# Sliding-window attention with own keys for each half block of 64 queries

## Chip, cores and metric

The kernel runs on one core of a Trainium2 chip. The metric is the device time of one execution in microseconds (us); lower is better. The time before is 763.34 us, the median of three runs (763.32 to 763.45).

## What is computed

An attention stage is followed by two mixture-of-experts layers. The inputs have 2 batches, 8 heads, 768 positions and a head dimension of 64. Each query sees the first 8 positions of its sequence (the global keys) and the 96 positions up to itself (the local keys), with a bias that grows with the distance:

```python
is_global = pos[None, :] < int(n_global)
is_local = (rel >= 0) & (rel < int(n_local))
dist = np.where(is_global & ~is_local, float(n_local), np.abs(rel))
scores = scale * q @ k.T - slopes[:, None, None] * dist
scores = np.where(is_global | is_local, scores, -1e9)
a = np.exp(scores - scores.max(-1)); a = a / (a.sum(-1) + 1e-9)
x = (a @ v)                       # then as rows of 8 * 64
idx = argmax(normalized(x) @ normalized(emb).T / tau)
x = gate[idx] * relu(x @ w1[idx]) @ w2[idx]          # layer 1, 8 experts
out = sum_e p[:, e] * relu(x @ w1[e]) @ w2[e]        # layer 2, 4 experts
```

## The kernel before

**Blocks.** The 1536 rows are 12 blocks (`T`) of 128 queries, six per batch. The 8 heads of a block are 4 pairs, called `n` in the code: 4 x t + 0 to 3, with the two heads `j` = 0, 1 of a pair on partitions 0 to 63 and 64 to 127 of queries and keys. The first block of a batch has only its own 128 keys. Every other block works on a window of 240: 96 local keys before the block and 16 slots for the global keys (`WG` = 112 together), and its own 128.

**One pair of one block** goes through these functions. `scores` (L541) multiplies queries by keys on TensorE, one matmul of 128 queries by 240 keys for each head. `maximum` (L554, VectorE) scales, adds the bias `biasw` and leaves the negated result in `aa` and the row's extreme in `nm`. `expo` (L560, ScalarE) takes the exponential and its row sum. `flip` (L568) transposes `aa` on TensorE in 128 by 128 squares, two for each head, four into one PSUM bank of the pool `ps_a`, which is then copied to SBUF as `ats` (L570, by ScalarE or VectorE as the call says). `av` (L582) multiplies by the values: for each head one matmul with the 112 keys of the earlier part (`vwin`) and one with the 128 own keys (`v`), accumulated in `o`, a bank of the pool `ps_o`.

**Finishing a block.** `fin0` copies `o` to `os` on ScalarE (L237). `fin_l` (L257) multiplies two pairs at a time by `idn`, which holds for every pair an identity and the expert embeddings side by side (144 columns): this puts the rows back in order and gives the expert logits, both in the one bank of the pool `ps_l`, called `lp`. VectorE reads it in `over_sums` (`lh`, L275) and `rows_x` (`xall`, L287), dividing by the row sums; `end_x` does both for one half. `choose` finds the expert of each row in small steps, `count` (L310, L311) and `fin2` (L317, L320) find each row's slot in the expert's list, and `scatter` (L324) writes the rows with an indirect DMA of the POOL queue to `xs` in DRAM, which must have been zeroed (`zero_fill`, L493, from `zt`).

**Order.** Each engine works through its own queue in program order, and the order is written out by hand in the loop over t at the end of the attention part: while block t has its flips, finishing of t-1 and weighted values, the scores of block t+2 follow on TensorE, and maximum and exponentials of block t+1 run on VectorE and ScalarE. PSUM's eight banks are divided among pools: `ps_o` 1, `ps_l` 1, `ps_a` 2, `ps_s` (scores) 4.

**Loads.** SyncE's queue issues them, also in program order: `load_v(t+2)` at the head of block t (L404 to L408), `load_kq(t+4)` (L389, L391), zero fills in blocks 1, 2, 4 and 5, and `load_to` (L86), which brings the first layer's weights (`raw`). `split_low_pieces` and `split_half` then split these weights in two parts, `wh` on ScalarE (L138, L141) and `wl` on POOL (L107) in this stage. `put_globals` (L396) copies the 16 global key slots behind each block's keys.

**The opening and the end.** `build_dist` (L476 to L478) and `build_biasw` (L482) make the distance and the eight biases on VectorE before block 1's maxima; `warm` issues matmuls that nobody reads. In the last block the lists of the last blocks are placed, 256 rows of the first expert are loaded from `xs` as `xe` (L699), and TensorE starts the first layer with `first_rows` (L360) and `add_rows` (L364).

Of the kernel before, what the change touches and what calls it, by code (L numbers as in the profile page):

```python
# [22 lines left out]
P = 128  # L23
GW = 16
PW = 96
WG = GW + PW
WIN = WG + 128
# [9 lines left out]
def tile_attention_moe_moe(ctx: ExitStack, tc: tile.TileContext, q, k, v, n_global, n_local,  # L37
# [169 lines left out]
    idn = cp.tile([P, NP, 2 * D + 2 * NE], F32, name="idn")  # L207
# [40 lines left out]
    HH, NX = H // 2, 2 * D + 2 * NE  # L248
    lps, pps = {}, {}

    def fin_l(t_, i, pool=None, place=None):


        pt = (pool or pl.l).tile([P, HP * NX + NE], F32, tag="at" if pool else "l", name="lp")
        lps[t_, i] = pt[:, 0:HP * NX].rearrange("p (a n) -> p a n", a=HP)
        for p_ in range(HP):
            nc.tensor.matmul(lps[t_, i][:, p_, :], osb[t_][:, i * HP + p_, :], idn[:, i * HP + p_, :],  # L257
                             start=True, stop=True)
        if place is not None:
            count(place, pt[:, HP * NX:])  # L260
# [8 lines left out]
    def over_sums(t_, i):  # L269

        rs, lh = osb[t_, 2]
        rp = rs.rearrange("p (i a j) -> p i a j", i=2, j=2)[:, i]
        lp = lps[t_, i]
        pt = lp[:, :, 2 * D:].rearrange("p a (j e) -> p a j e", j=2)
        nc.vector.tensor_tensor(lh[:, i * HH:(i + 1) * HH, :].rearrange("p (a j) e -> p a j e", j=2), pt,  # L275
                                rp.unsqueeze(3).to_broadcast([P, HP, 2, NE]), ALU.mult)

    def rows_x(t_, i, scalar=False):
        rs, _ = osb[t_, 2]
        rp = rs.rearrange("p (i a j) -> p i a j", i=2, j=2)[:, i]  # L280
        x_ = xall[:, t_, :].rearrange("p (i a j d) -> p i a j d", i=2, j=2, d=D)[:, i]
        pt = lps.pop((t_, i))[:, :, 0:2 * D].rearrange("p a (j d) -> p a j d", j=2)
        if scalar:
            for h in range(HH):
                nc.scalar.activation(x_[:, h // 2, h % 2], pt[:, h // 2, h % 2], AF.Copy, scale=rs[:, i * HH + h:i * HH + h + 1])
        else:
            nc.vector.tensor_tensor(x_, pt, rp.unsqueeze(3).to_broadcast([P, HP, 2, D]), ALU.mult)  # L287
# [79 lines left out]
    with ExitStack() as at:  # L367
# [4 lines left out]
        ap6 = at.enter_context(tc.tile_pool(name="ap6", bufs=6))  # L372
# [4 lines left out]
        pl.sb, pl.l = ap2, ps_l  # L377
# [4 lines left out]
        SEG = P + GW  # L382
        kp = [ap1.tile([P, NP, TB * SEG], F32, name=f"k{b}") for b in range(B)]
        vwin = [ap1.tile([WG, DM], F32, name=f"vwin{i}") for i in range(NB)]
        vt, qt = {}, {}
# [7 lines left out]
        def put_globals(b, i0, i1, copy=nc.gpsimd.tensor_copy):  # L393

            seg = kp[b].rearrange("p a (i c) -> p a i c", c=SEG)
            copy(seg[:, :, i0:i1, P:SEG],  # L396
                                  kp[b][:, :, 0:GW].unsqueeze(2).to_broadcast([P, NP, i1 - i0, GW]))

        def load_v(t_):
            b, i = divmod(t_, TB)  # L400
            s0 = i * P
            vw = vwin[t_ % NB]
            vt[t_] = ap3.tile([P, DM], F32, tag="v", name="v")
            nc.sync.dma_start(out=vt[t_], in_=v[b, s0:s0 + P, :])  # L404
            if i:
                nc.sync.dma_start(out=vw[0:PW], in_=v[b, s0 - PW:s0, :])
            if 1 <= i <= NB:
                nc.sync.dma_start(out=vw[PW:WG], in_=v[b, 0:GW, :])  # L408


        it32 = ap1.tile([P, WIN], I32, name="it32")
# [16 lines left out]
        nc.gpsimd.iota(it32[:, 0:PW], [[-1, PW]], base=PW, channel_multiplier=1)  # L428
# [175 lines left out]
        def end_x(t_, i):  # L604
            if t_ >= 0:
# [7 lines left out]
                if i:  # L613
                    choose(t_)
# [856 lines left out]
```

## Time and profile before

| what | value |
|---|---|
| median of three runs | 763.34 us |
| the profiled execution | 764.26 us, its span 762.5 us |
| granted TensorE clock, mean | 0.997 |
| busy share PE, DVE, ACT, POOL | 98, 75, 56, 46% |
| attention | from the start to about 92 us |
| the two layers | the rest |

PE is TensorE, PEld its weight loads, DVE VectorE, ACT ScalarE, POOL GpSimd, SP SyncE, which issues most DMAs. The span is the stretch that the profiler's records cover; the execution's own time is 1.76 us longer. The chain of waits is the chain of work that ended last, followed back from the last instruction. Rows of a timeline give start, duration, engine, line, operation, the tile written and the one read, shapes, and how many instructions the row holds; a bracket at the end gives the idle time before it and what ended that.

### The profile page before, as it was taken

The page shows a single profiled execution, that of the slowest core. Times are in us where ns is not written, and L with a number is a line of the kernel's source. Part 1 is how long each engine was busy: PE and PEld are TensorE (multiplying, and loading weights), DVE is VectorE, ACT ScalarE, POOL GpSimd, SP SyncE. Part 2 cuts the span into 40 slices and gives each one's busy share as a digit, 9 for nine tenths or more (in the row PEclk, how much of TensorE's full clock was granted, in tenths as well). Part 3 has the DMA queues.
Part 4 walks back from the last instruction along what each step waited for, and adds up shares of the span by engine and source line. Part 5 has one row for each costly group of instructions (what it writes and reads, how often), then busy time and mean ns, then how long its engine had stood idle before and what let it go on. Part 6 is the DMA issues. An engine that isn't in the chain of part 4 may idle for free.

```text
span 762.5 us, 16427 instructions
## 1 busy us (share of the span) xinstructions
PE 749.4 (98%) x6268; PEld 728.0 (95%) x6268; DVE 568.3 (75%) x1197; ACT 424.3 (56%) x865; POOL 349.2 (46%) x316
## 2 busy tenths in 40 slices
PE   8999999999999999999999999999999999999995
PEld 4888899999999999999999999999999999999995
DVE  6888676877979678777667678777677677766765
ACT  7899667766766565663444454444454344345331
POOL 2026450070004574676467366267357356555325
PEclk9999999999999999999999999999999999999998
DMA  7995467677797874566566566466557556644532
GB/s 230 324 304 203 136 218 237 213 235 245 259 325 258 314 268 157 210 251 238 186 249 248 193 245 238 171 236 245 194 183 264 194 205 229 223 170 173 213 132 96
DMA packets 46757, 169.89 MB, mean 223 GB/s; under 512 B 5368, under 2 KB 13576, under 8 KB 38208
## 3 DMA queue, kind: packets, MB, share of 16 engines
q1 hardware_dynamic: 44224, 162.11, 60.7%
q0 software_dynamic: 2416, 6.39, 2.3%
q8 instruction: 66, 1.08, 0.5%
q14 instruction: 35, 0.29, 0.1%
q10 hardware_dynamic: 16, 0.02, 0.0%
HBM read 146.96 MB, written 21.54 MB: 221 GB/s over the span
## 4 chain that ended last, share of the span: by engine, by line
PE 87%; DVE 4%; issue 4%; POOL 2%; ACT 1%; DMA 1%; POOLq 0%; SPq 0%; ACTq 0%; DVEq 0%
PE h L1091 10%; PE h L1092 10%; PE h L1093 10%; PE y L1172 6%; PE y L1170 6%; PE y L1171 6%; PE h L1019 3%; PE h L1020 3%; PE h L1021 3%; PE ya L1172 3%; PE ya L1171 3%; PE ya L1170 3%; PE ya L1039 3%; PE y L1039 3%; PE s L541 2%
## 5 line engine op out<-in xcount | busy, mean ns | idle before, releaser
L1091 PE MATMUL h<-xo,wt 128*128 128x256 f32 x672 | 190.4, 283 | 0.2 <-ACT h L1124 0.2
L1093 PE MATMUL h<-xo,wt 128*128 128x256 f32 x672 | 190.2, 283 | 0.0
L1092 PE MATMUL h<-xo,wt 128*128 128x256 f32 x672 | 190.2, 283 | 0.0
L157 POOL TENSOR_TENSOR wt<-raw,wt 128x512 fp32r<-128x512 f32 x75 | 101.6, 1355 | 142.8 <-ACT wt L156 142.8
L1091 PEld LDWEIGHTS h<-xo,wt 128*128 128x128 f32 x672 | 129.0, 192 | 0.5 <-ACT h L1124 0.4
L1092 PEld LDWEIGHTS h<-xo,wt 128*128 128x128 f32 x672 | 129.0, 192 | 0.0
L1093 PEld LDWEIGHTS h<-xo,wt 128*128 128x128 f32 x672 | 129.0, 192 | 0.0
L1072 DVE SCALAR_TENSOR_TENSOR xall<-y,rsb,xall 128x256 f32<-128x256 f32 x196 | 85.8, 478 | 52.8 <-PE y L1172 52.6
L1172 PE MATMUL y<-wt,hp 128*128 128x256 f32 x416 | 117.9, 283 | 0.1
L1170 PE MATMUL y<-wt,hp 128*128 128x256 f32 x416 | 117.7, 283 | 0.0
L1171 PE MATMUL y<-wt,hp 128*128 128x256 f32 x416 | 117.7, 283 | 0.0
L1096 ACT ACTIVATE hp<-hf 128x512 fp32r<-128x512 f32 x120 | 75.2, 628 | 57.8 <-DVE hf L1105 57.1
L1099 DVE TENSOR_TENSOR hp<-hf,hp 128x512 fp32r<-128x512 f32 x93 | 90.4, 976 | 0.0
L1172 PEld LDWEIGHTS y<-wt,hp 128*128 128x128 f32 x416 | 79.8, 192 | 0.5 <-DVE hp L1102 0.5
L1170 PEld LDWEIGHTS y<-wt,hp 128*128 128x128 f32 x416 | 79.9, 192 | 0.0
L1171 PEld LDWEIGHTS y<-wt,hp 128*128 128x128 f32 x416 | 79.9, 192 | 0.0
L94 DVE TENSOR_TENSOR wl<-raw,wh 128x1024 fp32r<-128x1024 f32 x60 | 76.8, 1295 | 0.1
L1138 ACT ACTIVATE hf<-h 128x512 f32<-128x512 f32 x24 | 14.3, 598 | 106.9 <-DVE h L1137 106.9
L124 ACT ACTIVATE wh<-raw 128x1024 fp32r<-128x1024 f32 x59 | 62.1, 1059 | 17.1 <-DMA raw<-in_moe_w_dram 13.2
L1170 PE MATMUL ya<-wt,hp 128*128 128x256 f32 x244 | 69.3, 284 | 0.1
L1171 PE MATMUL ya<-wt,hp 128*128 128x256 f32 x244 | 69.0, 283 | 0.0
L1172 PE MATMUL ya<-wt,hp 128*128 128x256 f32 x244 | 69.0, 283 | 0.0
(248 smaller groups left out, 1919.2 us busy)
## 6 DMA issues: line engine op xcount, KB each, us to landing
raw<-in_moe_w_dram SPq DMA_DIRECT2D x96, 512.0 KB, 4.6
xo<-xd SPq DMA_DIRECT2D x44, 1024.0 KB, 5.6
xo<-xd SPq DMA_DIRECT2D x22, 1536.0 KB, 6.2
xd<-xo SPq DMA_DIRECT2D x14, 512.0 KB, 5.1
xs<-zt SPq DMA_DIRECT2D x4, 1024.0 KB, 6.5
xr<-xs SPq DMA_DIRECT2D x14, 256.0 KB, 5.4
v<-in_v_dram SPq DMA_DIRECT2D x12, 256.0 KB, 4.5
k<-in_k_dram SPq DMA_DIRECT2D x11, 256.0 KB, 5.3
```

The costliest lines, as they stand in the source:

```text
L94: eng.tensor_tensor(lo, r, hi.bitcast(F32), ALU.subtract)
L124: nc.scalar.activation(hi, r, AF.Copy)
L157: eng.tensor_tensor(t[:, 1], src, t[:, 0].bitcast(F32), ALU.subtract)
L1072: nc.vector.scalar_tensor_tensor(a_, src, w_, a_, ALU.mult, ALU.add)
L1091: nc.tensor.matmul(pt[:, i], wh[:, d, ws], xh_[:, d], start=new and i == d == 0, stop=False, skip_group_check=True)
L1092: nc.tensor.matmul(pt[:, i], wh[:, d, ws], xl_[:, d], start=False, stop=False, skip_group_check=True)
L1093: nc.tensor.matmul(pt[:, i], wl[:, d, ws], xh_[:, d], start=False, stop=d == 1, skip_group_check=True)
L1096: nc.scalar.activation(parts[i][0], src, func)
L1099: eng.tensor_tensor(parts[i][1], src, parts[i][0].bitcast(F32), ALU.subtract)
L1170: nc.tensor.matmul(pt, hh[:, f, ts_], wh[:, f], start=new and f == 0, stop=False, skip_group_check=True)
L1171: nc.tensor.matmul(pt, hh[:, f, ts_], wl[:, f], start=False, stop=False, skip_group_check=True)
L1172: nc.tensor.matmul(pt, hl[:, f, ts_], wh[:, f], start=False, stop=f == 1, skip_group_check=True)
```

## The change

Each block of 128 queries is divided into two halves `g` of 64 (`HB`), and each half has its own window of 176 keys (`WIN` = 112 + 64): 112 earlier and global ones and its own 64. The second half's earlier keys are the first half's own 64, the 32 keys before them (the tail, `TL`) and the globals.

- **Scores**: tiles of 64 queries by up to 176 keys instead of 128 by 240; each pair has 9 matmuls (before 2), some of which cover two pieces. A tail of 32 keys is copied behind each block's keys by `put_tail` on POOL.
- **Bias**: `build_dist` has 13 VectorE instructions instead of 3, and makes the window for both heads, whose columns are in different order.
- **Flips**: `aa` of a pair is one row of 2 x 176 columns, so that the own keys of both heads lie together. Three squares are flipped for a pair instead of four: one for each head's 112, and one with both heads' own 64. `aa` lies in six fixed tiles.
- **Weighted values**: for each half and head one matmul of 64 x 64 with the 112 rows of `vh`, and one with the 128 rows of `vo`. `vo` holds the block's own values, each head on its half of the partitions and zeros on the other; `own_keys` copies it on POOL from `vh`, two copies of 64 x 512 a block.
- **Loads of values**: into three tiles `vh`, in two to five pieces a block; `load_v(t+2)` is called behind block t's `av` instead of at its head.
- **Finishing**: `fin_l` is called once a block, at its head, with 16 matmuls of 72 columns on tiles of 64 x 64 (before 4 of 144). The even heads go to `lp`, which is now a bank of `ps_a`, the odd ones to `lq`, a bank of `ps_o`'s tag. The pools are `ps_o` 1, `ps_a` 3, `ps_s` 4. `end_x` is one call, the odd heads first.
- **Order**: the maximum of `m1`'s second head is ahead of `end_x` and its exponential behind it; in odd blocks the copy of `n2`'s flip is VectorE's.

The two layers are not touched. The core of the diff:

```diff
-WIN = WG + 128
+HB = 64
+TL = PW - HB
+WIN = WG + HB
...
-    def fin_l(t_, i, pool=None, place=None):
-        pt = (pool or pl.l).tile([P, HP * NX + NE], F32, tag="at" if pool else "l", name="lp")
-        for p_ in range(HP):
-            nc.tensor.matmul(lps[t_, i][:, p_, :], osb[t_][:, i * HP + p_, :], idn[:, i * HP + p_, :],
-                             start=True, stop=True)
+    def fin_l(t_, place=None):
+        pt = [pool.tile([P, 512], F32, tag=tag, name=n) for (pool, tag), n in ((pl.l, "lp"), (pl.o, "lq"))]
+        for p_ in range(NP):
+            for j in range(2):
+                r0 = slice(D * j, D * j + D)
+                for g in range(2):
+                    c0 = slice(D * g, D * g + D)
+                    nc.tensor.matmul(lps[t_][j][c0, p_, :], osb[t_][r0, p_, c0], idn[r0, p_, :], start=True, stop=True)
...
-        ps_l = at.enter_context(tc.tile_pool(name="ps_l", bufs=1, space=PSUM))
-        ps_a = at.enter_context(tc.tile_pool(name="ps_a", bufs=2, space=PSUM))
+        ps_a = at.enter_context(tc.tile_pool(name="ps_a", bufs=3, space=PSUM))
...
+    def put_tail(t_):
+        b, i = divmod(t_, TB)
+        if i < TB - 1:
+            c0 = i * SEG
+            nc.gpsimd.tensor_copy(kp[b][:, :, c0 + P + GW:c0 + SEG], kp[b][:, :, c0 + HB - TL:c0 + HB])
...
+    def own_keys(t_):
+        if t_ % TB:
+            src = vh[t_ % NB][0:HB].rearrange("k g (a j d) -> k j g a d", j=2, d=D)
+            for j in range(2):
+                nc.gpsimd.tensor_copy(vo[HB * j:HB * j + HB, j], src[:, j])
...
-                    nc.tensor.matmul(score(n, j), qt[t_][r0, p_, :], kp[b][r0, p_, c1 - (WIN if i else P):c1], start=True, stop=True)
+                    elif j == 0:
+                        todo[j] = [(0, 0, c0 + HB, WIN), (1, HB, c0 + P - TL, GW + TL), (1, 0, c1, P)]
+                    else:
+                        todo[j] = [(0, HB, c0 + HB, WG), (1, P, c0 + P - TL, GW + TL), (0, 0, c1, HB),
+                                   (1, 0, c1 + HB, HB), (1, HB, c1, HB)]
+                while todo[0] or todo[1]:
+                    for j in range(2):
+                        for g, o, c, w in todo[j][0:2]:
...
+                            nc.tensor.matmul(s_, qt[t_][r0, p_, gs], k_, start=True, stop=True)
+                        del todo[j][0:2]
...
+                for j, c in enumerate((0, WIN + HB, WG)):
+                    nc.tensor.transpose(pt[:, j, :], a_[:, c:c + P], ident)
+                copy(s_, pt[:, 0:3, :])
...
+            for g in range(2):
+                gs = slice(HB * g, HB * g + HB)
+                for j in range(2):
+                    nc.tensor.matmul(o_[j][:, gs], vh[(t_ - 1 + g) % NB][0:WG, 1 - g, hs[j]], s_[0:WG, j, gs], start=True, stop=False)
+                for j in range(2):
+                    nc.tensor.matmul(o_[j][:, gs], vo[:, j, g, p_, :], s_[:, 2, gs], start=False, stop=True)
...
-            if 1 <= t_ and t_ + 2 < T:
-                load_v(t_ + 2)
+            if t_ + 2 < T:
+                put_tail(t_ + 2)
...
-                end_l(t_ - 1, 0)
+                end_l(t_ - 1)
                 top(m0, 0)
...
                 top(m1, 0)
-                flip(n2, nc.scalar.copy)
-                top(m1, 1)
-                end_x(t_ - 1, 0)
+                if t_ < T - 1:
+                    maximum(m1, 1)
+                end_x(t_ - 1)
...
+                flip(n2, nc.vector.tensor_copy if t_ % 2 else nc.scalar.copy)
+                if t_ < T - 1:
+                    expo(m1, 1)
                 tops(m2)
                 flip(n3, nc.vector.tensor_copy)
-                end_l(t_ - 1, 1)
                 tops(m3)
-                end_x(t_ - 1, 1)
             if t_:
                 for n in (n0, n1, n2, n3):
                     av(n)
...
+            if t_ and t_ + 2 < T:
+                load_v(t_ + 2)
+            if t_ + 1 < T:
+                own_keys(t_ + 1)
             if t_:
                 scores(2 * t_ + 4)
                 scores(2 * t_ + 5)
```

How it moves instructions is seen in three places. On TensorE one block before, from its scores to the count of the finished block (`s` scores, `at` flips, `lp` finishing):

```order
L541 MATMUL s<-k_127,q 128x240 x8
L568 MATMUL at<-ident,aa 128x128 x8
L257 MATMUL lp<-idn,os 128x144 x2
L568 MATMUL at<-ident,aa 128x128 x8
L257 MATMUL lp<-idn,os 128x144 x2
L310 LDWEIGHTS tri
L310 MATMUL lp<-oh,tri 128x8
```

TensorE in the same place now, first one pair's scores and the start of the finishing:

```order
L594 MATMUL s<-k_121,q 64x176
L594 MATMUL s<-k_121,q 64x48
L594 MATMUL s<-k_121,q 64x112
L594 MATMUL s<-k_121,q 64x48
L594 MATMUL s<-k_121,q 64x2x64
L594 MATMUL s<-k_121,q 64x64 x3
L262 MATMUL lp<-idn,os 64x72 x2
L262 MATMUL lq<-idn,os 64x72 x2
```

and from the finishing's end to the first weighted values (`o`):

```order
L312 LDWEIGHTS tri
L312 MATMUL lp<-oh,tri 128x8
L313 LDWEIGHTS ones
L313 MATMUL lp<-cum,ones 128x8
L623 MATMUL at<-ident,aa_130 128x128 x3
L623 MATMUL at<-ident,aa_131 128x128 x3
L623 MATMUL at<-ident,aa_132 128x128 x3
L623 MATMUL at<-ident,aa_133 128x128 x3
L646 MATMUL o<-ats,vh_124 64x64 x2
L648 MATMUL o<-ats,vo 64x64 x2
```

Both halves of the finishing and the count now stand ahead of all flips, and there are three flips for a pair. On POOL around the scatters of block 6, before:

```order
L324 DMA xs<-xall,slot 2048x512 x2
L107 TENSOR_TENSOR wl<-raw,wh 128x256 x4
L320 CAST slot<-base 128x1
L298 TENSOR_TENSOR cum<-cum,oh 128x8
L324 DMA xs<-xall,slot 2048x512 x2
```

and now:

```order
L430 COPY vo<-vh_124 64x512 x2
L326 DMA xs<-xall,slot 2048x512 x2
L109 TENSOR_TENSOR wl<-raw,wh 128x256 x4
L407 COPY k_122<-k_122 128x4x32
L322 CAST slot<-base 128x1
L300 TENSOR_TENSOR cum<-cum,oh 128x8
L430 COPY vo<-vh_125 64x512 x2
L326 DMA xs<-xall,slot 2048x512 x2
```

The copies for block 8's own keys (the second `vo`) stand behind two scatters and four weight pieces. On SyncE's queue in block 1, with what each instruction waits for (PE is TensorE), before:

```order
L404 DMA v<-in_v_dram 128x512 [waits DMAHW5_49,PE_49]
L406 DMA vwin_129<-in_v_dram 96x512 [waits DMAHW6_49]
L408 DMA vwin_129<-in_v_dram 16x512 [waits DMAHW7_49]
L389 DMA k_127<-in_k_dram 128x4x128 [waits DMAHW0_49]
L391 DMA q<-in_q_dram 128x512 [waits DMAHW1_49]
L493 DMA xs<-zt 512x1x512 [waits DMAHW2_49,DVE_49]
L86 DMA raw<-in_moe_w_dram 128x1024 [waits DMAHW3_49]
```

and now:

```order
L417 DMA vh_123<-in_v_dram 64x2x512 [waits DMAHW5_49,PE_49]
L418 DMA vh_123<-in_v_dram 32x512 [waits DMAHW6_49]
L420 DMA vh_123<-in_v_dram 32x512 [waits DMAHW7_49]
L392 DMA k_121<-in_k_dram 128x4x128 [waits DMAHW0_49]
L394 DMA q<-in_q_dram 128x512 [waits DMAHW1_49]
L531 DMA xs<-zt 512x1x512 [waits DMAHW2_49,DVE_49]
L88 DMA raw<-in_moe_w_dram 128x1024 [waits DMAHW3_49]
```

The order of the queue is the same, but the first load now waits for TensorE's weighted values of block 1 where it waited for those of block 0.

## Rows read from the trace of the kernel before

**Rows 1.** Windows: stretch, us, busy us (count) of each engine, PEclk, DMA share, GB/s.

```profile
30.00:40.00 10.00, 10.00 (x111) 8.81 (x108) 8.29 (x47) 9.39 (x32) 1.47 (x6) 1.00 0.92 304
```

**Rows 2.** Chain of waits in attention: start us, us, what.

```profile
30.71 1.82 PE s L541 x16
32.53 1.02 PE at L568 x8
33.56 0.49 PE lp L257 x4
34.05 0.95 PE at L568 x8
...
35.52 1.91 PE o L582 x32
37.43 1.82 PE s L541 x16
...
48.41 1.91 PE o L582 x32
...
67.27 1.91 PE o L582 x32
```

**Rows 3.** Timeline of VectorE in a full block.

```profile
43.14 0.19 DVE L275 TENSOR_TENSOR lh<-lp,rs 128x32 f32<-128x32 f32 x1
...
43.58 0.16 DVE L317 CUSTOM_DVE_ANT_0 g<-lp,oh 128x8 f32<-128x8 f32 x1
```

**Rows 4.** Timeline of VectorE in the opening.

```profile
9.21 0.34 DVE L476 TENSOR_SCALAR far<-rel,nf 128x240 f32<-128x240 f32 x1
...
10.03 0.23 DVE L478 TENSOR_SCALAR dd<-gf,nf 128x16 f32<-128x16 f32 x1
...
11.89 0.41 DVE L554 CUSTOM_DVE_ANT_0 aa<-s,biasw 128x240 f32<-128x240 f32 x1 [0.58 <-PE s L541]
```

**Rows 5.** Timeline of TensorE: block 0's second half of `fin_l`.

```profile
21.36 0.73 PE L257 MATMUL lp<-idn,os 128*128 128x144 f32 x4 [0.76 <-DVE xall L287]
```

**Rows 6.** SyncE's queue in block 1, then DMA issues of 10:20 (median us to landing).

```profile
16.04 0.33 SPq L404 DMA_DIRECT2D v<-in_v_dram  x1
...
19.30 0.62 SPq L86 DMA_DIRECT2D raw<-in_moe_w_dram  x1
...
raw<-in_moe_w_dram SPq DMA_DIRECT2D x1, 512.0 KB, 7.2
```

**Rows 7.** Timeline of ScalarE.

```profile
31.72 0.64 ACT L138 ACTIVATE wh<-raw 128x512 fp32r<-128x512 f32 x1
...
36.10 0.49 ACT L560 ACTIVATE aa<-aa,nm 128x240 f32<-128x240 f32 x1
```

**Rows 8.** Timeline of POOL.

```profile
3.29 0.61 POOL L433 COPY idn<-ident 128x512 f32<-128x512 f32 x1
...
58.11 1.12 POOL L324 DMA_INDIRECT xs<-xall,slot  x1 [0.70 <-issue]
...
83.64 2.79 POOL L107 TENSOR_TENSOR wl<-raw,wh 128x256 fp32r<-128x256 f32 x4
```

**Rows 9.** SyncE's queue in block 5, then the page's DMA issues (median us to landing).

```profile
44.19 0.33 SPq L404 DMA_DIRECT2D v<-in_v_dram  x1
...
47.64 0.57 SPq L493 DMA_DIRECT2D xs<-zt  x1
...
xs<-zt SPq DMA_DIRECT2D x4, 1024.0 KB, 6.5
```

**Rows 10.** Chain of waits at attention's end, then TensorE's timeline there.

```profile
86.83 2.73 DMA xs<-xall,slot
...
92.46 0.71 PE L360 MATMUL xy<-ident,xe 128*128 128x128 f32 x4 [0.45 <-DMA xe<-xs]
```

**Rows 11.** Timeline of TensorE: the last counts of attention.

```profile
91.78 0.17 PE L310 MATMUL pp<-oh,tri 128*128 128x8 bf16 x1
...
91.83 0.17 PE L760 MATMUL pp<-cum,ones 128*128 128x8 bf16 x1
```

More of the change, by code (lines that the diff above doesn't have):

```diff
@@ L563, in flip @@
         def flip(n, copy):
-            nh = 1 if n // NP % TB == 0 else 2
-            pt = ps_a.tile([P, 4, P], F32, tag="at", name="at")
-            for f in range(nh):
+            pt = ps_a.tile([P, 512], F32, tag="at", name="at").rearrange("p (a n) -> p a n", a=4)
+            s_ = ap4.tile([P, 3, P], F32, tag="ats", name="ats")
+            if n // NP % TB:
+                a_ = at_[n % 6]
+                for j, c in enumerate((0, WIN + HB, WG)):
+                    nc.tensor.transpose(pt[:, j, :], a_[:, c:c + P], ident)
+                copy(s_, pt[:, 0:3, :])
+            else:
@@ L567, in flip @@
                 for j in range(2):
[L568 to L571 removed]
+                    nc.tensor.transpose(pt[:, j, :], aa[n][:, j, 0:P], ident)
+                copy(s_[:, 0:2, :], pt[:, 0:2, :])
+            ats[n] = s_
         def av(n):
             t_, p_ = divmod(n, NP)
+            i = t_ % TB
@@ L575, in av @@
             if p_ == 0:
-                op_[t_] = ps_o.tile([P, NP, P], F32, tag="o", name="o")
-            s_, nh = ats.pop(n)
-            for f in range(nh):
-                vv, n = (vt[t_], P) if f == nh - 1 else (vwin[t_ % NB], WG)
-                for j in range(2):
-                    h = 2 * p_ + j
-                    nc.tensor.matmul(op_[t_][64 * j:64 * j + 64, p_, :], vv[0:n, h * D:(h + 1) * D], s_[0:n, 2 * f + j, :],
-                                     start=f == 0, stop=f == nh - 1)
@@ L585, in warm @@
-        def warm(n, pool=ps_a, tag="at"):
-            pt = pool.tile([P, 512], F32, tag=tag, name="pt")
+                op_[t_] = ps_o.tile([P, NP * P], F32, tag="o", name="o").rearrange("p (a n) -> p a n", a=NP)
+            hs = [slice((2 * p_ + j) * D, (2 * p_ + j + 1) * D) for j in range(2)]
+            o_ = [op_[t_][D * j:D * j + D, p_, :] for j in range(2)]
+            s_ = ats.pop(n)
+            if not i:
+                for j in range(2):
+                    nc.tensor.matmul(o_[j], v0[:, hs[j]], s_[:, j, :], start=True, stop=True)
+                return
@@ L588, in warm @@
+            for g in range(2):
+                gs = slice(HB * g, HB * g + HB)
+                for j in range(2):
+                    nc.tensor.matmul(o_[j][:, gs], vh[(t_ - 1 + g) % NB][0:WG, 1 - g, hs[j]], s_[0:WG, j, gs], start=True, stop=False)
+                for j in range(2):
+                    nc.tensor.matmul(o_[j][:, gs], vo[:, j, g, p_, :], s_[:, 2, gs], start=False, stop=True)
+        def warm(n):
+            pt = ps_a.tile([P, 512], F32, tag="at", name="pt")
             for _ in range(n):
@@ L589, in warm, with counts, end_l @@
                 nc.tensor.matmul(pt, zb[:, 0:P], zb, start=True, stop=True)
-        def counts(t_, i):
-            return 0 < t_ < T - 2 and i == (t_ < T - 3)
-        def end_l(t_, i):
-            if t_ >= 0:
-                fin_l(t_, i, place=t_ - 1 if counts(t_, i) else None)
+        def counts(t_):
+            return 0 < t_ < T - 2
+        def end_l(t_):
+            fin_l(t_, place=t_ - 1 if counts(t_) else None)
         def place_last(t_):
@@ L743, in tile_attention_moe_moe @@
                 split_half()
-        fin_l(T - 1, 0)
+        fin_l(T - 1)
         sum_up(T - 1)
@@ L750, in tile_attention_moe_moe @@
         rows_x(T - 1, 0, True)
-        fin_l(T - 1, 1, ps_a)
         over_sums(T - 1, 1)
```

166 lines of the change are left out of this document (93 added, 73 removed).

## The prediction

> **What bounds the kernel now.** I read the 10 us windows first, then the chain of waits, then single engines where the change puts work. [...] The stage after attention does the same work before and after, so what attention gains or loses is the whole difference. A difference of 0.2%, or 1.5 us, is about what a measurement of this kernel can tell from none.
>
> **The block, part by part.** *Flips*: 12 instead of 16. Sixteen take 1.02 + 0.95 = 1.97 [rows 2], so four fewer give 0.49 back. *fin_l*: before 8 matmul records of 144 columns in 0.98, 0.85 ns a column [rows 2]. Now 16 matmuls of 72 columns, that is 32 records, on four 64 by 64 tiles. The trace has no four tiles at once, so I bound it: four at once, 8 steps of 72 columns, 0.49; only two at once, as in the weighted values today, 0.98. The matmuls of one pair go to four different tiles, so I take 0.55 (gain 0.43). *Scores*: each tile now passes 176 columns twice per pair of heads. All four tiles at once: 4 x 2 x 176 x 0.85 ns = 1.20 us. But they are issued as 176, 48, 112, 48 columns, then 128, 64, 64, then 64 more, and a wide one holds up what comes behind it: without overlap of these three groups the widest add up to 368 columns, 2.50 us. I take the middle, 1.85, and 0.1 for starting three times as many instructions: 0.15 more than the 1.82 of now. *Weighted values*: 16 steps of 128 columns become 32 steps of 64, two tiles at a time: the same 1.91, and 0.1 for starting them. *A new wait*: `lp` of `fin_l` now lies in one of the three flip banks, so the third pair's flip must wait until VectorE has read it. VectorE takes 0.44 for one half of `lh` and `xall` (43.14 to 43.58) and 0.16 for the count's read [rows 3]: two halves and the read are 1.04, and I allow 0.25 for TensorE's last result and the two hand-overs. Against these 1.3 stand the 6 flips of two pairs that can go first, 0.74: TensorE stands for 0.55. Together -0.49 - 0.43 + 0.15 + 0.1 + 0.55 = -0.12 a block, and 8 blocks stand between the first full one and the tail: **-1.0 us**. With the bounds of scores and `fin_l` a block is between -0.8 and +1.0.
>
> ScalarE and VectorE gain more than TensorE: a block has 8 exponentials of 0.49 [rows 7] and as many biased minima, and all lose 64 of 240 columns, which I take as 0.05 to 0.07 each. With a quarter off its three flip copies and one of them given to VectorE in odd blocks, ScalarE's block falls from 6.3 (0.939 of 6.72) to about 5.4. That costs and gives nothing as long as TensorE's order ends last; it is the cover that two terms below eat.
>
> **The opening.** `build_dist` goes from 3 VectorE instructions to 13. The three take 1.0 us (9.21 to about 10.2); most of the new ones are narrower, so I price them at 0.2: 2.6, or 1.6 more. VectorE then waited 0.58 for scores [rows 4], which covers a part. The eight biases and eight minima that follow are 64 columns narrower (0.05 to 0.07 each, 0.9). And before, the second half of `fin_l` had to wait 0.76 for the one bank [rows 5]; now both halves have a bank. 1.6 - 0.58 - 0.9 - 0.76 is -0.6; `fin_l` itself is shorter as well: **-0.8** at the start of block 1's weighted values, bounds -1.5 and +1.0.
>
> **The SyncE queue.** `load_v(t+2)` moves from the head of block t to behind its weighted values, since its buffer is read there, and everything in that block's queue stands behind it. For block 1 that was: values issued at 16.04, then keys, queries, a zero fill and the first weight quarter at 19.30, which landed 7.2 later [rows 6], at 26.5. ScalarE wanted it at 31.72 [rows 7]. Now the queue waits for the end of the weighted values: 21.36 + 0.73 [rows 5] + 1.91 - 0.8 is 23.2, and 0.1 to see it; with the same 3.3 + 7.2 behind it the quarter lands at 33.8. ScalarE asks at 30.8 and stands, in order, for 3.0 us, with the exponentials and flip copies of two blocks behind it. At 5.4 of 6.6 us a block it regains 1.2, and TensorE's 0.55 lies in the same place: **+1.2**, bounds 0 and +3. Later quarters are split two blocks after their load and have room.
>
> **The POOL queue.** Each block gets two copies `vo` and one key tail. A POOL copy of 512 columns takes 0.61 [rows 8], so 1.2 and 0.25 a block. In the first half POOL is nearly empty. From block 6 on it also has two scatters (1.0 each and 0.3 ahead of them) and, every other block, 2.8 us of weight halves [rows 8]. The scatters must also wait for the last zero fill: before it was issued at 47.64, 3.45 after the values that head its block with five issues ahead of it, and lands 6.5 later [rows 9]. Now the queue waits for block 5's weighted values, 48.41 + 1.91 [rows 2] less 1.3 gained so far, 49.0; with seven issues ahead (3.45 x 7/5 = 4.8) it goes out at 53.8 and lands at 60.3, two us after the first scatter of now (58.11). Then 2.6 of scatters, 2.8 of halves, 0.5 of small work and 1.2 of copies: block 8's own keys are ready at 67.4, and TensorE wants them at 67.27 [rows 2] less 0.8, 66.5: **+1.1** with 0.2 for the hand-over, bounds 0 and +3.
>
> **The tail.** At the end the chain leaves TensorE: halves on POOL from 83.64, the scatter's transfer at 86.83 with its 2.73, then the load `xe`, for which TensorE waits 0.45 [rows 8, 10]. Now two copies for the last block (1.2) stand ahead of the halves. What TensorE gains in the last two blocks is not seen, and the start of `xe` moves by 1.2 less 0.1: **+1.1**, bounds +0.3 and +2.5.
>
> Sum: -0.8 - 1.0 + 1.2 + 1.1 + 1.1 = **+1.6 us**. The profiled execution took 764.26 (span 762.5), so 765.9; that execution stands 0.92 above the median of the three runs, 763.34, so the median should be **765.0**.
>
> **The rivals.**
> *Faster: the tiles overlap fully and the waits are covered.* Scores at 1.3 a block (-0.5) with the other terms as above is -0.6 a block, -4.8 over eight; opening -0.8; quarter and POOL 0.5 together; tail +1.1: -4.0, so 759.3. For it: pairs of tiles run at once today with almost no loss, 1.91 for 32 records of 128 columns. Against it: POOL and SyncE have the same work however fast TensorE is, and a faster TensorE meets them earlier.
> *No change: the two new waits do not come.* If the zero fill and the quarter land 2 us sooner than their medians, 2.3 goes: 762.7.
> *Slower by more: narrow matmuls cost more than their columns.* The closest to a smallest price is the end of attention, where the first and third of four matmuls of 8 columns start 0.05 us apart, 0.025 each [rows 11]. If 25 ns held between any two records, 32 of `fin_l` would take 0.8 (+0.25), and in the scores, where 10 of 16 records of a pair are 64 columns or less, some 0.35 more: +0.6 in each of 10 blocks, 771. It decides once a record of 64 columns takes longer than its 54 ns divided by the tiles at work. If only two tiles ran at once, the price is about the same (0.43 a block more).
> [...]
> *The change does not do what it says*: the third flip bank goes to `lp` in every block, so three banks may act as two; that is in the forecast as the 0.55.
>
> **How the numbers follow.** The forecast gets 0.43; its own range, 763 to 767.5, holds the spread of its five terms. Faster gets 0.22: the scores' lower bound is physical, but POOL, SyncE and VectorE stand close behind. No change gets 0.19, since both waits rest on landing times that scatter by 1 to 2 us. The expensive narrow matmul gets 0.16: the rows only show that 25 ns is possible, not that it is needed. Faster by over 0.2% (under 761.8): the 0.22 and 0.02 of the third case, 0.24. Within: the rest of the third and a quarter of the forecast, 0.28. Slower: 0.48. The range leaves out a tenth at each end: 760.0 to 770.0.
>
> **What would show it.** Right: a block period of about 6.6, with TensorE standing about 0.5 before the third pair's flips; one ScalarE wait of 2 to 3 us on `raw` near 31 us; a weighted-values stretch of block 8 broken by `vo`; `xe` waited for by more than 1 us. Wrong: a period under 6.2 (scores run on four tiles), or over 7 (narrow matmuls are dear); no wait on `raw`; scatters starting before 59 us.

## The result: 10.5 us slower, and the profile after

The changed kernel takes 773.93 us (median of 4 runs, 772.96 to 774.96) where the kernel before takes 763.39 beside it: a ratio of 1.0135 with an interval of [1.0116, 1.0154]. That is slower, as the forecast had it, but six times as much, and above the range of 760 to 770. The profiled execution has a span of 773.3 us against 762.5; the readings of this section are of that one execution.

The windows of the changed kernel (columns as in [rows 1]):

```profile
20.00:30.00 10.00, 9.01 (x302) 8.28 (x294) 8.81 (x53) 7.96 (x34) 1.83 (x5) 1.00 0.48 151
30.00:40.00 10.00, 5.97 (x143) 5.26 (x139) 4.67 (x27) 5.46 (x22) 2.29 (x6) 0.84 1.04 336
...
60.00:70.00 10.00, 7.50 (x223) 6.41 (x214) 7.14 (x42) 7.48 (x28) 2.66 (x5) 1.00 1.01 289
70.00:80.00 10.00, 5.70 (x127) 4.64 (x126) 5.28 (x30) 5.85 (x21) 8.61 (x17) 1.00 0.88 269
80.00:90.00 10.00, 8.75 (x237) 7.98 (x237) 5.06 (x29) 5.45 (x20) 6.31 (x11) 0.83 0.64 205
```

TensorE was busy for all of 30 to 40 us before [rows 1]; now it is for 5.97. In that stretch and from 60 to 80 the engines of the core all have time to spare, and only the DMA engines are full or nearly so (1.04, 1.01 and 0.88). TensorE has some 300 matmul records in an undisturbed window where it had 111.

The chain of waits in the same execution, with `s` scores, `at` flips, `o` weighted values:

```profile
23.99 1.39 PE s L594 x36
...
27.84 7.74 DMA raw<-in_moe_w_dram
...
63.97 0.61 POOL vo L430
64.58 0.56 SPq L88
65.26 4.62 DMA vh<-in_v_dram
69.88 0.98 POOL xs L326
...
74.84 0.62 POOL vo L430
...
78.32 2.77 issue
...
99.23 2.76 DMA xs<-xall,slot
...
102.18 2.68 DMA xe<-xs
```

Before, the chain ran through TensorE alone from 30.71 on in the blocks that [rows 2] shows. Now it leaves it for a weight quarter, for value loads, for POOL, and once for 2.77 us of "issue", time in which TensorE waited for nothing that the profile shows. TensorE's timeline at five places (`xy` is the first layer's first rows):

```profile
27.20 0.93 PE L623 MATMUL at<-ident,aa 128*128 128x128 f32 x6 [0.30 <-ACT ats L624]
...
71.01 0.28 PE L262 MATMUL lp<-idn,os 64*64 64x72 f32 x2 [1.95 <-issue]
...
74.83 0.33 PE L648 MATMUL o<-ats,vo 128*64 128x64 f32 x2 [1.00 <-POOL vo L430]
...
81.09 0.78 PE L594 MATMUL s<-k,q 64*64 64x176 f32 x12 [2.74 <-issue]
...
104.90 2.05 PE L362 MATMUL xy<-ident,xe 128*128 128x128 f32 x16 [0.84 <-DMA xe<-xs]
```

The first rows of the first layer start at 104.90, 12.4 us later than at 92.46 [rows 10]; 1.6 of that comes back in the layers. The 12.4 can be laid out by the starts of each block's weighted values. Undisturbed blocks (1 to 2, 9 to 11) follow each other after 6.15 us where it was 6.72 (37.43 less 30.71 in [rows 2]), so TensorE's own block is 0.57 shorter. With that, and with the shorter blocks around the change of batch as they are, the stretch from block 1 to block 11 would be 3.4 us shorter if nothing stood. Four intervals are longer (a stop is given here from the start of the last record before it to the start of the next, some 0.2 more than the idle time in the brackets above):

```text
blocks   undisturbed  measured   lost   what is in it
2 to 3      6.15       10.50     4.35   ScalarE waits 4.26 for raw
3 to 4      6.15        7.40     1.25   granted clock 0.50 from 36.8 to 40.2
7 to 8      6.15        9.63     3.5    own keys 1.3, a stop of 2.17 ("issue")
8 to 9      6.15       12.52     6.4    own keys 1.8, a stop of 2.98 ("issue"), granted clock 0.50 from 81.2 to 84.6
```

Together 15.4 lost, less 3.4, less 0.1 in the opening, plus 0.5 in the tail is 12.4. At the end of each of the two longest gaps, 4.3 and 2.98 us, the granted clock goes to 0.50 for 3.4 us. By estimate this costs 1.6 and 1.7, half of the 3.12 and 3.40 us that TensorE was busy in them; part of the first falls into the interval from 2 to 3.

```profile
36.80:40.20 3.40, 3.12 (x36) 2.79 (x38) 2.11 (x11) 3.12 (x13) 0.00 (x0) 0.50 1.05 413
81.20:84.60 3.40, 3.40 (x70) 3.26 (x71) 1.00 (x6) 0.06 (x1) 3.02 (x5) 0.50 0.79 246
```

The first loss was in the forecast. SyncE's queue stands until block 1's weighted values are through, and the first quarter is issued at 27.84, not 19.30 [rows 6]:

```profile
23.67 0.63 SPq L417 DMA_DIRECT2D vh<-in_v_dram  x1
...
27.84 0.63 SPq L88 DMA_DIRECT2D raw<-in_moe_w_dram  x1
...
62.73 0.56 SPq L531 DMA_DIRECT2D xs<-zt  x1
```

ScalarE, in order, stands for it:

```profile
35.61 0.63 ACT L140 ACTIVATE wh<-raw 128x512 fp32r<-128x512 f32 x1 [4.26 <-DMA raw<-in_moe_w_dram]
```

And the last zero fill, issued at 62.73 instead of 47.64 [rows 9], holds POOL's scatters, behind which stand the own keys of block 8:

```profile
68.45 1.12 POOL L326 DMA_INDIRECT xs<-xall,slot  x1 [3.22 <-DMA xs<-zt]
...
74.18 1.27 POOL L430 COPY vo<-vh 64x512 f32<-64x512 f32 x2
```

What was not in it are the stops in "issue". They are in the middle of rows of like matmuls whose operands are long there.

### The profile page after: what moved, and what is told of

It reads as the page before. It is cut to its first block, busy times and chain, and to the rows that moved or that the text cites. A ratio compares the mean times of both kernels' runs of the same rounds, so it can differ in the third digit from the quotient of the medians.

```text
span 773.3 us, 18680 instructions
## 1 busy us (share of the span) xinstructions
PE 744.8 (96%) x7348; PEld 723.2 (94%) x7348; DVE 563.5 (73%) x1212; ACT 414.7 (54%) x860; POOL 367.7 (48%) x354
## 4 chain that ended last, share of the span: by engine, by line
PE 83%; issue 4%; DMA 4%; DVE 3%; POOL 3%; ACT 3%; SPq 0%; POOLq 0%; ACTq 0%; DVEq 0%
PE h L1157 10%; PE h L1159 10%; PE h L1158 10%; PE y L1238 6%; PE y L1237 6%; PE y L1236 6%; PE h L1085 4%; PE h L1086 4%; PE h L1087 4%; PE ya L1236 3%; PE ya L1238 3%; PE ya L1237 3%; PE y L1105 3%; PE ya L1105 3%; DMA raw<-in_moe_w_dram 2%
## 5 line engine op out<-in xcount | busy, mean ns | idle before, releaser
L96 DVE TENSOR_TENSOR wl<-raw,wh 128x1024 fp32r<-128x1024 f32 x60 | 73.5, 1240 | 0.2 <-ACT wh L126 0.2
```

The lines of the kernel that those rows point to most:

```text
L96: eng.tensor_tensor(lo, r, hi.bitcast(F32), ALU.subtract)
```

## The experiments

Four theories, named by letters. **Q**: SyncE's queue stands behind the weighted values, and its late loads are the loss. **P**: POOL's copies and scatters bound the second half. **N**: narrow matmuls are dear. **F** came up with the first runs: TensorE stands for its own instructions.

### Four single edits

The first quarter one block earlier:

```diff
-                    load_to(min(nxt[1] + RAW, t_))
+                    load_to(min(nxt[1] + RAW, max(t_, 1)))
```

> The changed kernel with one load moved: the first weight quarter is issued at the end of block 0, ahead of block 1's value loads. Theory Q (SyncE's queue stands behind the weighted values): ScalarE's wait of 4.26 us on raw goes, and with it block 3's late start; the third block period falls from 10.5 to about 6.2, and if nothing later takes it back the time is 774 - 5 = 769. Theory P (POOL: own keys, tails and scatters bound the second half whatever comes before): the gap at 31 us closes, but blocks 7 to 9 end where they ended, 773 to 774. Theory N (narrow matmuls are dear): the undisturbed period is what costs, the wait is hidden, 773 to 774 with a period over 6.7.

Four value tiles, with the loads at the block's head (memory from the queries' pool and from `sqe`):

```diff
-        NB = 3
+        NB = 4
-            if t_ and t_ + 2 < T:
-                load_v(t_ + 2)
...
         for t_ in range(T):
+            if 1 <= t_ and t_ + 2 < T:
+                load_v(t_ + 2)
```

> The changed kernel with a fourth value tile, so that the value loads of block t+2 stand at the head of block t as before the change (the memory comes from one query buffer fewer and a shared scratch tile; nothing else). Theory Q: no load waits for the weighted values of its own block any more; the raw wait goes, the last zero fill is issued 4 to 8 us sooner, and the stalls of blocks 7 to 9 shrink with it: every block near the undisturbed 6.15, about 774 - 4.3 - 1.2 - 7 = 761. Theory P: only the raw wait goes, about 769. Theory N: no more than 1 us.

Earlier zero fills:

```diff
-        ZF = (1, 2, 4, 5)
+        ZF = (1, 2, 3, 4)
-                if ready and t_ > ZF[-1]:
+                if ready and t_ > 5:
```

> The changed kernel with the zero fills in blocks 1, 2, 3 and 4 instead of 1, 2, 4 and 5; the scatters still begin in block 6. Theory Q: the raw wait at 31 us stays, but POOL's wait of 3.2 us for the last fill (68.45) goes, and what stands behind it there: 2 to 4 us less, 770 to 772. Theory P: the whole knot of blocks 7 to 9 hangs on POOL's late start, 7 us less, 767. Theory N: no change.

And the kernel before with its `load_v(t_ + 2)` moved behind `av`:

> The kernel before the change with one call moved, the value loads of block t+2 from the head of block t to behind its weighted values, as the change has it; tiles, scores, flips and POOL's work as before. Theory Q: this alone makes ScalarE wait for raw (about 4 us near 31 us) and the loads of later blocks late: 766 to 770 against 763.4. Theory P: POOL has none of the copies here, so only the raw wait shows and is partly regained, 763.5 to 765. Theory N: 763.4, no difference.

Measured: 774.44 (769.71 to 775.76), 770.86 (767.08 to 772.99), 769.94 (768.09 to 773.21) and 763.14 us, beside 763.56 for the kernel before. The variants scatter by 5 to 6 us where the kernel before has 1.3, so 3 or 4 us between two of them are hardly told apart, and a trace shows one execution only. With the quarter ahead, the raw wait is gone and nothing is gained. The chain of that run shows what came in its place:

```profile
33.61 0.99 issue
...
38.81 2.82 issue
```

With value loads ahead the raw wait is gone too, and there is a stop in the middle of block 2's weighted values:

```profile
29.27 2.66 issue
```

So Q's late loads are real, but another thing limits TensorE in the same place. With early fills there is no stop over 0.6 us from 65 to 86 us, and blocks 7 to 10 follow each other after 6.15 to 6.20. The fourth run was no test: the moved call is issued in the same order behind the same buffers, and its first load still goes out at 16.04 as in [rows 6]. In the changed kernel the wait comes from the buffer and not from the place of the call alone: block t still reads the value tile of block t-1, into which those of t+2 go.

### Where TensorE stops

The page's DMA queues have a row for instructions (packets, MB, share). Of the kernel before:

```profile
q8 instruction: 66, 1.08, 0.5%
```

Of the changed kernel:

```profile
q8 instruction: 75, 1.23, 0.6%
```

Each is one packet of 16,384 bytes. If I number TensorE's records in order of time, weight loads, matmuls and the few semaphore and branch instructions alike, and list the stops without a shown wait that end 1.1 to 1.8 us after such a packet, they fall on these numbers (in brackets the length in us, from start to start):

```text
after          2753 (2.17)  3009 (2.98)
quarter ahead  1217 (1.26)  1473 (3.09)  2753 (2.60)  3009 (2.99)
values ahead    961 (2.88)  1217 (2.06)  1985 (1.59)  2241 (0.76)  3009 (2.49)
early fills    1985 (0.98)  2241 (0.83)
fin_l in 8     1985 (2.58)  2497 (1.93)  2753 (0.97)
```

All are 705 + 256 k, in programs whose other queues differ, and in the last line (a run below) in one whose blocks have 32 instructions fewer, so that the stops fall on other operations. 16,384 bytes by 256 is 64 bytes an instruction. From 10 to 100 us the changed kernel has 15 such packets for 14.6 pieces of 256 records, the kernel before 7 for 7.2. So in these traces TensorE's instructions come by DMA during the run in pieces of 256, and it stops at the end of a piece when the next is not there: in the changed kernel for 2.17 us at 2753 and for 2.98 at 3009.

A block had about 150 such records in 6.72 us before, so a piece lasted some 11 us. Now it has 350 in 6.15: 4.5 us. How long a fetch waits, if it is asked for when the piece before it begins (no record shows the asking), and how full the DMA engines were meanwhile:

```text
run, piece      piece begun  fetch ran       waited  DMA share  stop
after 1985         48.2      48.51 to 49.94   0.3      0.37      none
after 1217         29.3      34.69 to 35.94   5.4      1.01      under the raw wait
after 2753         65.6      68.52 to 69.40   2.9      1.01      2.17
after 3009         71.0      78.29 to 79.49   7.3      0.82      2.98
ahead  961         24.1      29.13 to 30.31   5.0      1.02      2.88
```

In these rows the fetch with the engines 0.37 busy runs after 0.3 us, and those with them at 0.82 to 1.02 wait 3 to 7 us; to this come 0.9 to 1.4 of its own and 1.1 to 1.8 to the next matmul. The five are chosen. All 172 fetches of the attention stage in the traces of the changed kernel and its 14 variants, measured in the same way, show a tendency and not a rule:

```text
DMA share while waiting   fetches   waited: median, range   stops over 0.6 us
under 0.5                    29        0.6   -0.1 to 1.9            1
0.5 to 0.95                  56        1.8    0.4 to 7.3           11
0.95 and more                87        3.2    0.6 to 5.6           42
```

In these traces full engines make a long wait likely (a median of 3.2 us), not certain: in the changed kernel itself the fetches for 2241, 3265 and 3521 waited only 1.95, 1.10 and 1.02 at a share of 0.98 to 1.02. The earliest fetches start within about 0.1 us of the begin of the piece before; there the asking cannot have been later. What a fetch stands behind no record shows, so the waits of 3 to 7 us are measured and not explained.

### Fewer or more instructions

The kernel before with narrower matmuls, four for each score matmul and two for each of `fin_l` and `av`:

```diff
-                    nc.tensor.matmul(score(n, j), qt[t_][r0, p_, :], kp[b][r0, p_, c1 - (WIN if i else P):c1], start=True, stop=True)
+                    w = WIN if i else P
+                    for c in range(0, w, w // 4):
+                        nc.tensor.matmul(score(n, j)[:, c:c + w // 4], qt[t_][r0, p_, :], kp[b][r0, p_, c1 - w + c:c1 - w + c + w // 4], start=True, stop=True)
```

> The kernel before the change with narrower matmuls and nothing else: each score matmul in four pieces, each of fin_l and of the weighted values in two, the columns and the work the same. TensorE then has about 320 instructions a block where it had 150 (the changed kernel has 350); SyncE's and POOL's queues are untouched. Theory F (the instructions of TensorE come by DMA, 16 KB at a time, and such a fetch queues behind the data when the DMA engines are full): TensorE stands for 1 to 3 us several times, each time about 1.4 us past the end of an instruction fetch, with no wait shown: 767 to 772. Theory Q and theory P: no late load and no late copy here, so 763.4 to 764.5. Theory N: every block longer, by up to 0.6 us, with no single stop: 765 to 769.

The changed kernel with half the matmuls in `fin_l`:

```diff
-                for g in range(2):
-                    c0 = slice(D * g, D * g + D)
-                    nc.tensor.matmul(lps[t_][j][c0, p_, :], osb[t_][r0, p_, c0], idn[r0, p_, :], start=True, stop=True)
+                nc.tensor.matmul(lps[t_][j][:, p_, :], osb[t_][r0, p_, :], idn[r0, p_, :], start=True, stop=True)
```

> The changed kernel with fin_l in 8 matmuls of 64 rows by 128 columns where it has 16 of 64 by 64: 32 of 350 TensorE instructions a block fewer, everything else the same. Theory F: the stops come a little later and are shorter, -1 to -4 us: 770 to 773. Theories Q and P: 773.9 within 0.5, as TensorE's block alone is not what ends last. Theory N: up to 0.3 a block less, 771.

Both missed, and in a way of their own: 821.33 us (810.77 to 821.88) and 778.51 (776.74 to 779.29). The narrow pieces keep their weights 128 columns wide, and loading these seems to be what takes the time. A window of the kernel before in narrow pieces has the weight loads (third column) busy for 9.81 of 10 us:

```profile
55.00:65.00 10.00, 10.00 (x162) 9.81 (x161) 5.43 (x31) 6.35 (x21) 1.09 (x4) 1.00 0.58 203
```

and its chain has 64 score records in 4.51 us, 70 ns each, where the changed kernel has its 64 (8 matmuls a pair, two records each, and not the 9 matmuls named under the change) on four tiles in about 1.4, 22 ns each:

```profile
57.15 4.51 PE s L544 x64
```

So its block is 10.2 us, a piece of 256 lasts some 8, and no stop of theory F comes. The run does not show whether 320 instructions starve TensorE in 6.7 us. That it has no stops may come from the longer piece or from the DMA engines, which are only 0.58 busy in that window. `fin_l` in 8 lengthens the undisturbed block from 6.15 to 6.69. That run took 4.6 us more than the changed kernel (1.4 of it stands in the kernel before beside it, too), where F had 1 to 4 less. Its stops, 2.58, 1.93 and 0.97, are no shorter than before, since they land in other places. Theory N is right for wide weights and wrong for the tiles of the change.

### Edits together

`fin_l` in 8, first quarter ahead and early fills; then the same with the fourth value tile:

> The changed kernel with the first quarter ahead, the zero fills in blocks 1 to 4 and fin_l in 8 matmuls together. Theory Q: both late loads are gone, so 774 - 5 - 4 = 765. Theory F: the transfers are still as many and bunch up in the first 50 us, so stops of TensorE after fetches stay there; the second half is free of them as in the run with the early fills: 765 to 769.

> The same three edits with the fourth value tile and the value loads at the head of the block. Theory Q: nothing late is left, every block at 6.15: 760 to 761. Theory F: loads that go out sooner fill the DMA engines sooner, so the fetches of the first 45 us wait as long; 763 to 767.

The first two edits with `fin_l` as it was; value loads last in the block's queue (`load_v(t_ + 2)` behind `load_to`); the same with early fills; early fills with the fourth value tile:

> The changed kernel with the first quarter ahead and the zero fills in blocks 1 to 4; fin_l stays at 16 matmuls, since 8 of them cost 0.54 a block more. Theory F: stops of TensorE remain, all at instruction 705 + 256 k, in the first 50 us, where all transfers now bunch up, and none in the second half: 764 to 767. Theory Q: no late load is left that TensorE or ScalarE waits for, so every block 6.15: 760 to 762.

> The changed kernel with the value loads moved to the very end of each block's queue, behind keys, queries, zero fill and weights, which so no longer stand behind the weighted values. The DMA engines, idle from 20 to 23.5 us in the changed kernel, then have work there. Theory F: raw wait gone, transfers spread better, fewer stops: 766 to 770. Theory Q: raw wait gone and keys and queries early: 762 to 764; only the value loads are late. Theory P: the own keys come later with their values, 770 or more.

> The same with the zero fills in blocks 1 to 4 as well. Theory F: the second half is free of stops as in the run with early fills, the first keeps one or two: 762 to 766. Theory Q: 760 to 762.

> The changed kernel with four value tiles, the value loads at the head of the block, and the zero fills in blocks 1 to 4. Theory Q: 760 to 761, every block at 6.15. Theory F: the DMA engines are busy without a pause from 20 to 60 us, so stops of 2 to 3 us at 961 or 1217 stay: 764 to 768.

Measured 770.42, 775.67 (770.97 to 779.09), 774.64 (769.99 to 780.71), 783.30, 782.89 and 776.68 us, beside 764.78 (first two) and 765.44 for the kernel before. Every forecast of Q is off by 5 us or more. For value loads last P had 770 or more, and that holds: the loads of `vh` now come late, and with early fills TensorE stands 4.51 us for `vo` before 77.91. Each of these runs has stops on 705 + 256 k (in the last 960, 1216 and 1472, 2.1 to 2.6 us each; one record is missing in that trace), as F says; F's times are too low as well, by 1.4 us in the first run and by 8 to 17 in the others.

### Fewer bytes

The weight quarters paced, with three and four value tiles, and in the kernel before:

```diff
-                    load_to(min(nxt[1] + RAW, t_))
+                    load_to(min(nxt[1] + RAW, (1, 1, 1, 2, 2, 3, 4, 5, 7, 9)[t_]))
```

> The changed kernel with the weight quarters paced: the first at the end of block 0, the second in block 3, the third in block 5, then one or two a block, so that 1 MB fewer is moved in blocks 2 to 4. Theory F, with full DMA engines as the reason for late fetches: the stops before 55 us get rarer and shorter, and the raw wait is gone: 765 to 769. Theory Q: only the raw wait counts: 769. If the fetches are late for another reason: stops as before, 773 or more.

> The same with the fourth value tile and the value loads at the head of the block. Theory F: nothing waits for late loads and the DMA engines have room, so most blocks run at 6.15: 760 to 766. Theory Q: 760 to 761. If the fetches are late for another reason: stops of 2 to 3 us as in the run with value loads ahead, 768 to 771.

> The kernel before the change with the weight quarters paced in the same way, the control: TensorE never stands for instructions there, so 763 to 765 like the kernel before beside it, by every theory.

784.46, 780.40 and 765.22 us (the kernel before beside them 765.89). F had 765 to 769 and 760 to 766 for the first two, and missed both. In the first the pacing itself failed: a later quarter now goes out behind value loads that stand, and the chain has it for 9.38 us:

```profile
52.64 6.57 DMA vh<-in_v_dram
59.23 9.38 DMA raw<-in_moe_w_dram
```

In the second, from 20 to 60 us, the DMA share is 0.91 (0.97 with value loads ahead and all quarters early) and TensorE is busy for 34.23 us (31.69), as F says, but blocks 6 to 9 follow each other after 8.9 to 9.3 us, and only part of that is stops on 705 + 256 k; the rest stays open.

So the last runs leave transfers out instead. Their later blocks compute with the keys and queries of earlier ones, so only the attention stage is compared:

```diff
-            nc.sync.dma_start(out=kp[b][:, :, i * SEG:i * SEG + P], in_=k[b, :, :, i * P:(i + 1) * P])
+            if b == 0:
+                nc.sync.dma_start(out=kp[b][:, :, i * SEG:i * SEG + P], in_=k[b, :, :, i * P:(i + 1) * P])
+            if t_ > 3:
+                qt[t_] = qt[t_ - 4]
+                return
```

> The changed kernel without the key loads of the second batch and without the query loads from block 4 on: the first batch's keys and four blocks' queries are used again, so rows of later blocks are other rows and the experts' loads differ; only the attention stage is compared, by the start of the first layer's first rows (92.5 us before, 104.9 in the changed kernel). TensorE's instructions are the same. Theory F with full DMA engines: some 0.5 MB fewer a block, so fetches wait 1 to 2 us and not 3 to 7, stops are gone but for one or two before 45 us, and the start comes at 92 to 98. If fetches are late for another reason: stops as before and 102 to 105. Theory Q: value loads still stand behind the weighted values, the raw wait stays at about 4 us.

> The same loads left out, with the fourth value tile and the value loads at the head of the block. Theory F with full DMA engines: no stop over 1 us, every full block 6.15 to 6.3, the first rows at 88 to 91, ahead of before. If fetches are late for another reason: stops of 2 to 3 us at 961 and 1217 as in the run with value loads ahead, first rows at 99 to 102.

> The kernel before the change with the same loads left out, the control: its blocks are 6.72 of TensorE's own time with 0.94 of the DMA engines, so fewer loads change nothing in attention: first rows at 92 to 92.6, by every theory.

The first rows start at 99.47, 96.98 and 93.17 us: 5.4 sooner than in the changed kernel, 4.7 sooner than with value loads ahead (101.63), and 0.7 later in the control, whose blocks are 6.72 as ever. The first two lie between what F (92 to 98, 88 to 91) and its rival (102 to 105, 99 to 102) gave. In the first ScalarE still waits 3.1 us for `raw`, and three stops are left, 0.88, 0.92 and 2.44, where the changed kernel had 2.17 and 2.98 and one under the raw wait. The window from 20 to 60 us of the kernel with value loads ahead and all loads:

```profile
20.00:60.00 40.00, 31.69 (x882) 27.54 (x872) 27.11 (x167) 27.79 (x105) 11.41 (x28) 0.96 0.97 290
```

The same window with fewer loads:

```profile
20.00:60.00 40.00, 35.26 (x1006) 30.27 (x995) 32.42 (x196) 32.37 (x124) 14.04 (x33) 1.00 0.78 248
```

The DMA share falls from 0.97 to 0.78 and TensorE is busy 3.6 us more. Its fetches, by the table's measure, wait 0.9 to 2.3 us but for three, which wait 3.1 to 5.4 with the DMA engines at 1.01 to 1.04; two others at 1.05 and 1.06 wait 1.6 and 1.1. The five stops listed for values ahead, 9.8 us in all, are down to three: 704 (0.76), 960 (1.37) and 3008 (2.72), 4.9 in all (one record is missing in this trace, too). So here fewer bytes beside the fetches went with fewer and shorter stops, which supports full DMA engines as the reason; F's time (88 to 91) does not hold, since the chain of this run goes over to POOL at 57 us:

```profile
57.16 0.61 POOL vo L434
...
58.61 1.12 POOL xs L326
60.03 0.99 POOL xs L326
61.09 2.80 POOL wl L109 x4
...
65.26 0.61 POOL vo L434
```

There P is right: scatters, weight halves and own keys are what the chain goes through as soon as TensorE no longer ends last.

No version beat the kernel before. What the runs leave open is one that has the shorter block and both fewer bytes in blocks 1 to 5 and less on POOL, and when a fetch is asked for.

## Why the prediction was wrong

- **The sign was right, the size and the main reason were not.** Forecast 765.0, measured 773.93. The sign came as a small rest of terms that nearly cancel (3.4 of losses against 1.8 of gains); in the traces both sides are larger, 15.9 against 5.1 with the 1.6 of the layers. Of the signs it named, a period under 6.2, a sign of being wrong, came true; the wait on `raw` came, longer than named, block 8 was broken by `vo`, and `xe` was waited for by 0.84 and not by more than 1.
- **The block**: forecast 0.12 shorter, measured 0.57. The scores' middle value, 1.85 and 0.1 for starting, was the wrong choice: they take 1.39, close to the lower bound of 1.20 for four tiles at once. `fin_l` takes about 0.7 (0.55), the weighted values 1.9 as said. The third pair's flips start 0.57 after the last of the second pair, 0.30 of it idle, where 0.55 was forecast. But the profile names ScalarE's copy of the first pair as what they wait for, not VectorE's reading of `lp` (only in block 7 it names VectorE).
- **Narrow matmuls**: the rival of 25 ns a record gave 771 and a longer block. The block is shorter, at 22 ns a score record of 48 to 176 columns on four tiles. That the time came out beyond 771 has another ground.
- **The opening**: 0.1 gained, not 0.8. The longer `build_dist` took what the bank gave.
- **The SyncE queue**: right in mechanism, +1.2 in size; 4.35 and 1.25 were measured. ScalarE waited 4.26 and not 3.0, and nothing was regained, as the granted clock fell to 0.50 at 36.8 us, while TensorE stood, and a fetch was late in the same place: without the raw wait two stops, 4.4 us together, took its room.
- **The POOL queue**: right in place (own keys of block 8 behind the scatters and the last fill), +1.1 in size, 9.9 measured over two blocks. Of these the own keys are 3.1 (1.8 in block 8, where 1.1 was forecast, and 1.3 in block 7), the two stops 5.2, and the granted clock of 0.50 behind them most of the rest. The fill went out at 62.73, not 53.8: the loads at its queue's head were 5 us late (53.88, not 49.0), and the way from them to the fill took 8.9 and not 4.8.
- **The tail**: +0.5 where +1.1 was forecast; it hides behind a later TensorE.
- **The step that failed** is the price of "three times as many instructions": 0.1 us a block for starting them. Their supply was put at nothing, and the runs show that it is what stops TensorE: 2.17 and 2.98 us at the ends of two pieces of 256 instructions, and 4.4 more, earlier on, in the run where the raw wait is taken away. The rows for it were there: 0.92 of the DMA engines busy [rows 1] entered no term, and the page lists the packets of the instructions beside those of the data. The second step that failed is the size of the SyncE term, 1.2 against 5.6 measured. How the 10.5 us divide between supply and late loads is not shown, since no run is free of the stops.

## What to carry to other kernels

Before a change that cuts matmuls into more and narrower ones, work out how long TensorE takes for 256 of its instructions (weight loads count), and look at how full the DMA engines are in the same stretch: here, at some 4.5 us and a share of 0.95 or more, 42 of 87 fetches had a stop of over 0.6 us; at 11 us and a share of 0.9 to 1.0, in the kernel before, no gap at the end of a piece was over 0.3 (nor were there stops at 8 us, but there the share was 0.58). A stop that the profile calls "issue", in the middle of like instructions, was told apart here by its place: count the records and look for steps, which were 256 in these traces. And where one engine gains, price what the others have to deliver in the shorter block as a whole, in bytes and POOL time per block, not wait by wait.

## What the runs showed of the hardware that was not expected

- TensorE's instructions were fetched during the run, 16,384 bytes for 256 (75 packets in the changed kernel), on a DMA queue of their own; a fetch ran 0.3 us after the piece before it began with the DMA engines 0.37 busy; over 87 fetches with them at 0.95 or more the median was 3.2 us, from 0.6 to 5.6.
- Tiles of 64 by 64 worked at the same time: 64 score records of 48 to 176 columns, 5,632 together, took about 1.4 us. One after another, at the 0.85 ns a column of `fin_l` in [rows 2], they would take 4.8: by estimate 3.4 tiles at once. With weights of 128 columns in front of 60-column matmuls it was 70 ns a record.
- At the end of a stand of 4.3 us, and again after one of 3.0 (start to start), the granted clock was 0.50 for 3.4 us in the changed kernel.
